# Copies of transposed keys and queries: four neighbouring words written at a time

## The chip, the cores and the metric

The program runs on one core of a Trainium2 chip. The metric is the device time of one execution in microseconds, and each kernel is given as the median of its runs. The core has a matrix engine (TensorE, PE in the profile, with its weight loads as PEld), a vector engine (VectorE, DVE), a scalar engine (ScalarE, ACT), GpSimd (POOL) and a queue engine (SyncE, SP) that issues transfers. Each engine takes its instructions in program order and waits on semaphores for the others. [...]

## The reference

```python
# B, H, S, D = 4, 8, 768, 48
mag = np.sqrt(a_re * a_re + a_im * a_im)
scale = np.minimum(mag, 0.999) / (mag + 1e-06)
a_re_n, a_im_n = (a_re * scale, a_im * scale)
for t in range(S):
    new_re = ar * S_re - ai * S_im        # ar, ai: step t of a_re_n, a_im_n
    new_im = ar * S_im + ai * S_re
    S_re, S_im = (new_re + k[t] (outer) v[t], new_im)
    y[:, :, t] = q[t] @ S_re
x = y as 3072 tokens of 384
h = x @ w_in                    # 384 x 2048
g = h * clip(h + 3, 0, 6) / 6
x = g @ w_out                   # 2048 x 384
h = x @ w_in2
g = max(h, 0) + alpha * min(h, 0)
out = g @ w_out2
```

A recurrence with complex decay per head feeds two feed-forward layers over 3072 tokens.

## The kernel before

**Work.** The 4 x 768 steps of the recurrence are handled in 12 groups of 256 tokens, each of two chunks of 128. For each group VectorE and ScalarE normalise the decay (`norm_ops`), multiply it up along time (`scan_ops`) and scale keys and queries by it, which gives the tiles `Kt` and `A`. Then `chunk_ops` does each chunk as masked attention on TensorE: transposes of keys and queries, scores `ps`, the masked product `PT`, outputs `py`, and the update `pu` of the running state `W`. The rows `xr` of a group are split into two parts (`xT`, `split_x`), and `ffn` runs the feed-forward layers: 16 steps a layer, each with matmuls into `ph` (L658), a gate on ACT and DVE (L670 to L680) that gives `gs`, and matmuls into `acc` (L695). The weights are decoded from 64-bit words once (`split_w`, `decode_f64`, mostly on DVE), stored, and fetched again for later passes (`fetch_w`).

**Order.** A list of positions (`Timeline`) sets the program order. Each group's attention steps are spread over a stretch of positions, and in between stand the steps of a feed-forward pass of earlier groups. In the first two groups there is no or little feed-forward work to stand there.

**Around the change.** A chunk's tokens lie in the tiles so that a token is t x 8 + j: 16 values of t and 8 heads give the 128 partitions, and j is the first free dimension. The helper `tr` (L563 to L568) transposes four of the eight j of one chunk with four TensorE transposes (L566) into one PSUM tile `pt` of 96 partitions x 4 x 128 words, and one ACT copy (L567) brings that to SBUF, to `KTr` or `QT`, whose 128 columns of a head are in the order of time (t outside, j inside). Each chunk has four such steps (keys half 0 and 1, queries half 0 and 1), so there are 96 copies. `pt` has one buffer (pool `ps1`, `bufs=1`), so that the next four transposes wait until the copy has read it:

```python
pt = ps1.tile([P, 4, P], F32, tag="pt", name=f"pt{n}_{g}_{half}")
...
ops += [kt0, lambda: tr(Kt, KTr, 1), lambda: tr(Qt, QT, 0), lambda: tr(Qt, QT, 1)]
```

The tag `pt` is also used for the two transposes `ptt` of `totals` (L412), for `pe` (L492) and for `gx` (L601).

Of the kernel before, what the change touches and what calls it, by code (L numbers as in the profile page):

```python
# [28 lines left out]
TB, J = 16, 8  # L29
# [190 lines left out]
def recurrence_ffn_kernel(ctx: ExitStack, tc, al, qkl, vl, w1, w2, alpha, q, k, v, a_re, a_im, out):  # L220
# [8 lines left out]
    D2 = 2 * D  # L229
# [108 lines left out]
    def grp(n):  # L338
        return divmod(n, NG)
# [213 lines left out]
    def chunk_ops(n, g, xr):  # L553
        b, cp_ = grp(n)
        c = G * cp_ + g
        Qt, Kt, V = Q_t[n], K_t[n], V_t[n]
        QT = lp.tile([D2, H, C], F32, tag="QT", name=f"QT{n}_{g}", bufs=2)
        KTr = lp.tile([D2, H, C], F32, tag="KT", name=f"KT{n}_{g}")
        KN = lp.tile([P, H, D2], F32, tag="KN", name=f"KN{n}_{g}")
        PT = [lp.tile([P, 4, C], F32, tag="PT", name=f"PT{n}_{g}_{i}", bufs=2) for i in range(2)]  # L560
        ops = []

        def tr(src, dst, half):  # L563
            pt = ps1.tile([P, 4, P], F32, tag="pt", name=f"pt{n}_{g}_{half}")
            for jj in range(4):
                nc.tensor.transpose(pt[:D2, jj], src[:, 4 * half + jj, g].rearrange("p c d -> p (c d)"), ident)  # L566
            nc.scalar.copy(  # L567
                dst.rearrange("p h (t j) -> p j (h t)", j=J)[:, 4 * half : 4 * half + 4], pt[:D2]  # L568
            )

        def natural():
            if c < NCH - 1:
                for h in range(H):
                    nc.sync.dma_start(
                        KN[:, h],
                        Kt[TB * h : TB * (h + 1), :, g].rearrange("p j c d -> p j (c d)"),
                    )

        def kt0():
            natural()  # L580
            tr(Kt, KTr, 0)

        ops += [kt0, lambda: tr(Kt, KTr, 1), lambda: tr(Qt, QT, 0), lambda: tr(Qt, QT, 1)]

        def scores(i):
            ps = ps1.tile([P, 4, C], F32, tag="ps", name=f"ps{n}_{g}_{i}")
            for hh in range(4):
                h = 4 * i + hh
                nc.tensor.matmul(ps[:, hh], lhsT=KTr[:, h], rhs=QT[:, h], start=True, stop=True)  # L589
            nc.vector.tensor_mul(PT[i], ps, mask.unsqueeze(1).broadcast_to([P, 4, C]))  # L590

        ops += [lambda: scores(0), lambda: scores(1)]

        def update():
            if c == NCH - 1:
                return
            pu = ps1.tile([P, H, D], F32, tag="ps", name=f"pu{n}_{g}")
            for h in range(H):
                nc.tensor.matmul(pu[:D2, h], lhsT=KN[:, h], rhs=V[:, g, h], start=True, stop=True)  # L599
            gx = ps1.tile([P, H], F32, tag="pt", name=f"gx{n}_{g}")  # L600
            nc.tensor.matmul(  # L601
                gx[:D2], lhsT=sel[:, g].rearrange("p c d -> p (c d)"), rhs=gam_t[n], start=True, stop=True
            )
            W = lp.tile([D2, H, D], F32, tag="W", name=f"W{n}_{g}", bufs=2)
            gb = gx[:D2].unsqueeze(2).broadcast_to([D2, H, D])
            if c == 0:
                nc.scalar.copy(W, pu[:D2])
            else:
                nc.vector.tensor_add(W, W_t[n, g], pu[:D2])
            if n < WACT:  # L610
                gs_ = lp.tile([D2, H], F32, tag="gsb", name=f"gsb{n}_{g}")
                nc.scalar.copy(gs_, gx[:D2])
                for h in range(H):
                    nc.scalar.activation(W[:, h], W[:, h], AF.Copy, scale=gs_[:, h : h + 1])
            else:
                nc.vector.tensor_mul(W, W, gb)
            W_t[(n, 1) if g == 0 else (n + 1, 0)] = W

        def outputs():
            for hp in range(H // 2):  # L620
                for par in range(2):
                    h = 2 * hp + par
                    o = py[64 * par : 64 * par + D, hp]
                    nc.tensor.matmul(o, lhsT=V[:, g, h], rhs=PT[h // 4][:, h % 4], start=True, stop=(c == 0))  # L624
                    if c > 0:
                        nc.tensor.matmul(o, lhsT=W_t[n, g][:, h], rhs=QT[:, h], start=False, stop=True)  # L626
            ys = lp.tile([P, 4, C], F32, tag="ys", name=f"ys{n}_{g}")
            nc.scalar.copy(ys, py)
            tk = slice(g * C, (g + 1) * C)
            for par in range(2):  # L630
                nc.sync.dma_start(xr[D * par : D * (par + 1), :, tk], ys[64 * par : 64 * par + D, 0:3])
            for par, e0, kk, p0, m in ((0, 0, 0, 96, 32), (0, 32, 1, 96, 16), (1, 0, 1, 112, 16), (1, 16, 2, 96, 32)):
                nc.sync.dma_start(xr[p0 : p0 + m, kk, tk], ys[64 * par + e0 : 64 * par + e0 + m, 3])

        ops += [outputs, update]
        return ops
# [212 lines left out]
```

## Time and profile before

| | before |
|---|---|
| median of 3 runs | 1198.31 us (1196.89 to 1199.21) |
| the profiled execution | 1198.93 us, of which its span 1197.2 us |
| PE busy | 1031.2 us (86%) |
| PE weight loads busy | 846.9 us (71%) |
| DVE busy | 802.1 us (67%) |
| ACT busy | 615.3 us (51%) |
| DMA, mean | 163 GB/s |

The span is the time from the first to the last instruction of the profiled execution; the time of the run has 1.7 us around it. The busy shares are means over stages that have different limits: for the first 60 us there is almost no TensorE work, later TensorE is busy nearly all the time. PE intervals are pipelined and their ends are modelled, so consecutive PE rows can overlap by some 0.2 us.

### The profile page before, as it was taken

The numbers are of one execution on the slowest core, as the hardware profiler recorded it, in microseconds if no ns is written. First come the engines' busy times: TensorE is split into PE (matmuls) and PEld (weight loads), VectorE is DVE, ScalarE is ACT, GpSimd is POOL, SyncE is SP. The second block draws the span as 40 slices with busy tenths as digits, with TensorE's granted clock in tenths as the row PEclk, the third lists the DMA queues.
The fourth block names the chain that finished last, engine by engine and source line by source line (L and its number), as shares of the span: only waits on it lengthen the run. The fifth ranks groups of instructions, "written<-read, shape, count | busy, mean of one in ns | idle before, by whom it ended". The sixth has DMA issues, their size and how long they took to land.

```text
span 1197.2 us, 15796 instructions
## 1 busy us (share of the span) xinstructions
PE 1031.2 (86%) x5914; PEld 846.9 (71%) x5914; DVE 802.1 (67%) x1537; ACT 615.3 (51%) x1003; POOL 2.0 (0%) x13
## 2 busy tenths in 40 slices
PE   0026946979998789999999999999999999999997
PEld 0015935957787787777878778778788777788786
DVE  7985973999895586948738749559579375333432
ACT  5453634667665455755356564446554346432433
POOL 0000000000000000000000000000000000000000
PEclk9999876999999899999999999999999999999999
DMA  8642472476575675445534544543454344244430
GB/s 339 253 167 61 142 303 67 134 275 194 222 247 181 213 243 178 134 128 174 171 102 153 171 120 158 193 136 116 131 188 139 130 124 138 89 163 134 133 129 30
DMA packets 70500, 194.60 MB, mean 163 GB/s; under 512 B 29456, under 2 KB 38672, under 8 KB 70416
## 3 DMA queue, kind: packets, MB, share of 16 engines
q1 hardware_dynamic: 70272, 193.50, 48.6%
q8 instruction: 49, 0.80, 0.3%
q14 instruction: 35, 0.29, 0.1%
q10 hardware_dynamic: 144, 0.01, 0.0%
HBM read 158.08 MB, written 22.81 MB: 151 GB/s over the span
## 4 chain that ended last, share of the span: by engine, by line
PE 66%; DVE 16%; ACT 12%; DMA 3%; issue 2%; SPq 0%; DVEq 0%; ACTq 0%
PE ph L658 27%; PE acc L695 24%; PE ps L589 5%; PE pt L566 4%; ACT KT L567 4%; ACT QT L567 4%; PE pu L599 3%; PE py L624 2%; DVE w L294 2%; DVE wd L76 2%; DVE wd L77 2%; PE py L626 2%; DMA w<-wsd 1%; DVE gs L680 1%; DMA A<-in_al_dram 1%
## 5 line engine op out<-in xcount | busy, mean ns | idle before, releaser
L695 PE MATMUL acc<-gs,w 128*128 128x512 f32 (+1 forms) x2016 | 453.3, 366 | 7.2 <-ACT gs L679 4.8
L695 PEld LDWEIGHTS acc<-gs,w 128*128 128x128 f32 x2016 | 335.2, 188 | 69.2 <-ACT gs L679 7.3
L658 PE MATMUL ph<-xT,w 128*128 128x256 f32 (+1 forms) x1152 | 231.2, 348 | 20.9 <-ACT xT L550 14.9
L658 PE MATMUL ph<-xs,w 128*128 128x512 f32 x864 | 224.3, 401 | 3.2 <-DVE xs L704 2.5
L658 PEld LDWEIGHTS ph<-xT,w 128*128 128x128 f32 x1152 | 185.1, 197 | 50.8 <-ACT xT L550 16.0
L658 PEld LDWEIGHTS ph<-xs,w 128*128 128x128 f32 x864 | 158.3, 188 | 40.6 <-DVE xs L704 4.0
L679 ACT CAST gs<-r 128x512 fp32r<-128x512 f32 x192 | 119.7, 624 | 119.6 <-DVE r L671 71.6
L680 DVE TENSOR_TENSOR gs<-r,gs 128x512 fp32r<-128x512 f32 x192 | 132.0, 689 | 63.5 <-ACT gs L679 63.4
L678 DVE SCALAR_TENSOR_TENSOR r<-n,nal,r 128x512 f32<-128x512 f32 x96 | 71.9, 749 | 80.9 <-ACT n L675 80.5
L670 ACT ACTIVATE r<-ph 128x512 f32<-128x512 f32 x96 | 57.3, 597 | 129.2 <-PE ph L658 128.7
L671 DVE SCALAR_TENSOR_TENSOR r<-r,ph 128x512 f32<-128x512 f32 x96 | 65.7, 684 | 83.4 <-ACT r L670 82.9
L674 ACT ACTIVATE r<-ph 128x512 f32<-128x512 f32 x96 | 57.5, 599 | 83.9 <-PE ph L658 83.1
L567 ACT COPY KT<-pt 96x512 f32<-96x512 f32 x48 | 54.8, 1143 | 47.6 <-PE pt L566 39.4
L590 DVE TENSOR_TENSOR PT<-ps,mask 128x512 f32<-128x512 f32 x48 | 33.2, 692 | 62.7 <-PE ps L589 61.0
L589 PEld LDWEIGHTS ps<-QT,KT 96*128 96x128 f32 x384 | 54.5, 214 | 21.8 <-ACT QT L567 18.5
L589 PE MATMUL ps<-QT,KT 96*128 96x128 f32 x384 | 60.5, 307 | 10.7 <-ACT QT L567 9.7
L567 ACT COPY QT<-pt 96x512 f32<-96x512 f32 x48 | 54.8, 1142 | 21.5 <-PE pt L566 21.5
L566 PE MATMUL pt<-ident,Kt 128*96 128x128 f32 x192 | 33.1, 298 | 38.0 <-DVE Kt L518 30.5
L675 ACT ACTIVATE n<-ph 128x512 f32<-128x512 f32 x96 | 57.4, 598 | 0.0
L566 PEld LDWEIGHTS pt<-ident,Kt 128*96 128x96 f32 x192 | 22.6, 136 | 48.6 <-ACT wd L73 21.2
L566 PE MATMUL pt<-ident,A 128*96 128x128 f32 x192 | 33.8, 303 | 20.9 <-ACT QT L567 10.3
L566 PEld LDWEIGHTS pt<-ident,A 128*96 128x96 f32 x192 | 20.9, 135 | 38.7 <-ACT QT L567 19.0
(107 smaller groups left out, 1054.0 us busy)
## 6 DMA issues: line engine op xcount, KB each, us to landing
w<-wsd SPq DMA_DIRECT2D x139, 768.0 KB, 4.4
raw<-in_w_dram SPq DMA_DIRECT2D x32, 768.0 KB, 5.7
wsd<-w SPq DMA_DIRECT2D x23, 768.0 KB, 4.1
A<-in_al_dram SPq DMA_DIRECT2D x12, 768.0 KB, 4.6
qk<-in_qkl_dram SPq DMA_DIRECT2D x12, 768.0 KB, 5.4
KN<-Kt SPq DMA_DIRECT2D x160, 48.0 KB, 2.3
v<-in_vl_dram SPq DMA_DIRECT2D x12, 384.0 KB, 4.4
out_dram<-o SPq DMA_DIRECT2D x18, 256.0 KB, 3.2
```

Source lines behind the costliest of these rows:

```text
L566: nc.tensor.transpose(pt[:D2, jj], src[:, 4 * half + jj, g].rearrange("p c d -> p (c d)"), ident)
L567: nc.scalar.copy(dst.rearrange("p h (t j) -> p j (h t)", j=J)[:, 4 * half : 4 * half + 4], pt[:D2])
L589: nc.tensor.matmul(ps[:, hh], lhsT=KTr[:, h], rhs=QT[:, h], start=True, stop=True)
L658: nc.tensor.matmul(ph_, lhsT=w[:, wl, kk], rhs=x[:, xl, kk], start=(kk == 0 and wl == 0 and xl == 0), stop=(kk == KT - 1 and wl == 1),)
L670: nc.scalar.activation(r, ph_, AF.Relu, bias=0.5, scale=1.0 / 6.0)
L671: nc.vector.scalar_tensor_tensor(r, r, 1.0, ph_, op0=ALU.min, op1=ALU.mult)
L674: nc.scalar.activation(r, ph_, AF.Relu)
L675: nc.scalar.activation(neg, ph_, AF.Relu, scale=-1.0)
L678: nc.vector.scalar_tensor_tensor(r[:, k], neg[:, k], nal[:, ii : ii + 1], r[:, k], op0=ALU.mult, op1=ALU.add)
L679: nc.scalar.copy(gs[:, 0], r)
L680: nc.vector.tensor_sub(gs[:, 1], r, gs[:, 0].bitcast(F32))
L695: nc.tensor.matmul(acc, lhsT=w[:, wl, e * P : (e + 1) * P], rhs=gs[:, gl], start=(i == 0 and wl == 0 and gl == 0), stop=(i == NF - 1 and g ...
```

## The change

The ACT copy of `tr` reads and writes the same words as before and puts each to the same place. Only the order in which it walks them differs. Before, the outer loop is j (four) and the inner loop the 128 columns of one transpose: it reads PSUM in four runs of 128 neighbouring words, and each word is written 8 words (32 bytes) behind the one before. After, the outer loop is the 128 columns and the inner loop the four j: it writes runs of four neighbouring words (16 bytes), with 32 bytes from one run to the next, and reads each word of a run 128 words (512 bytes) behind the one before, in PSUM.

```diff
             nc.scalar.copy(
-                dst.rearrange("p h (t j) -> p j (h t)", j=J)[:, 4 * half : 4 * half + 4], pt[:D2]
+                dst.rearrange("p h (t j) -> p (h t) j", j=J)[:, :, 4 * half : 4 * half + 4],
+                pt[:D2].rearrange("p j x -> p x j"),
             )
```

The number of instructions and their order are as before on every engine; on ACT only the shape of the 96 copies is another (96x128x4 for 96x4x128). Lines behind L567 have a number that is higher by one.

## Rows read from the trace of the kernel before

**Rows 1.** The page's head and its part 1, busy time by engine.

```profile
span 1197.2 us, 15796 instructions
PE 1031.2 (86%) x5914; PEld 846.9 (71%) x5914; DVE 802.1 (67%) x1537; ACT 615.3 (51%) x1003; POOL 2.0 (0%) x13
```

**Rows 2.** Stretches: length, busy us (instructions) by engine, PE clock, DMA share, GB/s.

```profile
60.00:240.00 180.00, 119.55 (x849) 108.67 (x850) 131.15 (x251) 89.23 (x153) 0.00 (x0) 0.86 0.44 146
240.00:480.00 240.00, 213.38 (x1458) 181.74 (x1457) 191.61 (x372) 141.44 (x240) 0.00 (x0) 0.99 0.65 218
480.00:1080.00 600.00, 586.27 (x3133) 467.56 (x3132) 389.23 (x748) 312.52 (x499) 0.00 (x0) 1.00 0.45 143
```

**Rows 3.** Shares of the chain that ended last, by line, from the page.

```profile
PE ph L658 27%; PE acc L695 24%; PE ps L589 5%; PE pt L566 4%; ACT KT L567 4%; ACT QT L567 4%; PE pu L599 3%; PE py L624 2%; DVE w L294 2%; DVE wd L76 2%; DVE wd L77 2%; PE py L626 2%; DMA w<-wsd 1%; DVE gs L680 1%; DMA A<-in_al_dram 1%
```

**Rows 4.** Groups of ACT by shape: count, busy us, mean ns, idle before, releaser.

```profile
L567 ACT COPY KT<-pt 96x512 f32<-96x512 f32 x48 | 54.8, 1143 | 47.6 <-PE pt L566 39.4 <-PE ps L589 8.0
L567 ACT COPY QT<-pt 96x512 f32<-96x512 f32 x48 | 54.8, 1142 | 21.5 <-PE pt L566 21.5
L73 ACT ACTIVATE wd<-raw 128x768 f32<-128x768 f32 x32 | 29.1, 911 | 19.3 <-DVE w L294 16.8 <-DMA raw<-in_w_dram 2.4
...
L628 ACT COPY ys<-py 128x512 f32<-128x512 f32 x24 | 14.1, 587 | 33.7 <-PE py L626 26.0 <-PE py L624 5.6 <-DMA w<-wsd 1.8
...
L528 ACT ACTIVATE Ts<-Ts 128x768 f32<-128x768 f32 x12 | 10.1, 845 | 0.1
```

**Rows 5.** Line L567, 60 to 240 us: durations, and who waited (us, times).

```profile
L567 ACT COPY KT<-pt x8: 1069/1092/1100, 79.3 to 187.8; 96x512 f32<-96x512 f32 x8
...
  PE pt L566: 13.3, 11
...
  PE ps L589: 4.6, 4
```

**Rows 6.** The same line, 240 to 480 us: who waited.

```profile
  PE pt L566: 5.8, 15
...
  PE ps L589: 2.0, 5
```

**Rows 7.** The same line, 480 to 1080 us: durations, and who waited.

```profile
L567 ACT COPY KT<-pt x28: 1132/1155/1247, 508.4 to 1034.0; 96x512 f32<-96x512 f32 x28
...
  PE pt L566: 7.7, 23
  PE ps L589: 3.0, 8
...
  PE ptt L412: 1.1, 3
```

**Rows 8.** Timeline of PE around one copy: start, length, what, idle before, releaser.

```profile
622.79 1.18 PE L695 MATMUL acc<-gs,w 128*128 128x512 f32 x4
624.28 0.64 PE L566 MATMUL pt<-ident,A 128*96 128x128 f32 x4 [0.31 <-ACT KT L567]
```

**Rows 9.** Timeline of ACT at the same place.

```profile
623.07 1.16 ACT L567 COPY KT<-pt 96x512 f32<-96x512 f32 x1 [0.77 <-PE pt L566]
```

**Rows 10.** The chain in order of time, a stretch with no wait: start, length, what.

```profile
640.15 2.10 PE acc L695 x9
```

**Rows 11.** Timeline of PE in the first group's attention.

```profile
82.78 1.09 PE L566 MATMUL pt<-ident,A 128*96 128x128 f32 x4 [1.19 <-ACT KT L567]
```

**Rows 12.** Waits of PE, 130 to 200 us: in total, times, longest.

```profile
PE pt L566 <- DVE Kt L518: 9.7, 1, 9.7
```

**Rows 13.** A stretch of the weight decoding, columns as in the second group.

```profile
240.00:300.00 60.00, 50.62 (x285) 38.82 (x284) 56.78 (x83) 42.24 (x70) 0.00 (x0) 1.00 0.69 234
```

**Rows 14.** Waits of PE for the copies, 240 to 300 us: in total, times, longest.

```profile
PE pt L566 <- ACT QT L567: 0.7, 2, 0.3
PE pt L566 <- ACT KT L567: 0.3, 1, 0.3
```

## The prediction

> **What bounds the kernel now.** I read the busy times first: PE is busy 86% of the span, more than any other engine [rows 1]. Then the stretches, because that share is a mean over stages. From 480 to 1080 us PE is busy 586.27 of 600 us at a granted clock of 1.00: TensorE sets the pace, and what it loses there, 13.7 us in all, lengthens the program. From 60 to 240 us it is busy only 119.55 of 180 us, and between 240 and 480 us 213.38 of 240 us, so other things hold it up there [rows 2]. The chain that ended last says where the copies stand: keys and queries take 4% of the span each, some 96 us, although the 96 copies last only 109.6 us altogether (54.8 and 54.8) [rows 3, 4]. So nearly every copy is on the path.
>
> Next, the groups by shape. A copy takes 1143 ns for 512 words of 96 partitions; the copy of `py` at L628, which also moves 512 words a partition from PSUM to SBUF but reads and writes them side by side, takes 587 ns [rows 4]. The 556 ns between them are 1.09 ns for each word that is written 32 bytes behind the last one. That is what the change goes for.
>
> Last, who waits for the copies. PE idles for them 13.3 + 4.6 = 17.9 us in 15 waits from 60 to 240 us [rows 5], 5.8 + 2.0 = 7.8 us in 20 waits from 240 to 480 us [rows 6], and 7.7 + 3.0 + 1.1 = 11.8 us in 34 waits from 480 to 1080 us [rows 7]: there it is most of the 13.7 us that PE loses.
>
> **What one wait is worth.** At 622.79 four matmuls of the feed-forward start, and the transposes behind them start at 624.28 [rows 8]. Without a wait nine such matmuls take 2.10 us, 0.233 each [rows 10], so the transposes could start at 622.79 + 4 x 0.233 = 623.72: 0.56 us are lost, though the row says 0.31 idle, since the modelled end of a matmul lies behind the time at which the next could start. The copy runs from 623.07 to 624.23 [rows 9]. A copy shorter by up to 0.56 us thus gives all of it back to this wait. In the first groups the wait is longer, 1.19 us, because nothing stands between two sets of transposes [rows 11]: there any shortening counts in full.
>
> **The cost of a copy after.** No row shows an engine that reads PSUM in steps, so I bound it from both sides.
> - Write side: with four words side by side, at best nothing is left of the 556 ns; at worst each of the 128 jumps still pays 1.09 ns, 0.14 us.
> - Read side, below: nothing, 0.587 us for the copy, the duration of L628. A price below that has no reason: it moves as many words a partition.
> - Read side, above: each word read 512 bytes behind the last pays what a word written in steps pays now, 1.09 ns: 0.587 + 0.556 = 1.14 us, as before. It could be more; that is the slower rival below.
> - Nearest row of a read in steps on ACT: the activation at L73 takes every second word of `raw`, 911 ns for 768 words, against 845 ns for the one at L528, which reads them side by side [rows 4]. That is 66 ns, 0.086 ns a word, 0.045 us for 512.
>
> I take that row, since it is the same engine and the same side of the instruction, though it reads SBUF and in steps of 8 bytes: 0.587 + 0.045 = 0.63 us. A copy gets shorter by 1.155 - 0.63 = 0.52 us in the late stretch, by about 0.51 from 240 to 480, and by 1.08 - 0.63 = 0.45 in the early one, where those of keys take 1.07 to 1.10 us [rows 5, 7].
>
> For the write side the rows above show only the price of single words at 32 bytes. [...]
>
> [...] The read now is in four runs of 128 neighbouring words, and no row shows one in steps. [...]
>
> **The sum.**
> - 480 to 1080 us: 34 waits x 0.52 = 17.7 us. At least the idle time shown, 11.8.
> - 240 to 480 us: VectorE is busy 56.78 of the 60 us up to 300 us, among other things with decoding weights [rows 13], so I count nothing for the three waits of that stretch, 0.7 + 0.3 us [rows 14]; the other 17 give 17 x 0.51 = 8.7 us. At least their idle time, 7.8 - 1.0 = 6.8.
> - 60 to 240 us: 15 waits x 0.45 = 6.8 us. Between the first two groups TensorE waits 9.7 us for `Kt` from VectorE [rows 12]. VectorE takes its work in order and itself waits for scores in the first group's attention, so it should get ahead by the same time and hand most of it on; if it does not, half is lost, 3.4.
> - After 1080 us no copy is left (the last of keys starts at 1034.0 [rows 7]). No other instruction changes. ACT is freed of some 50 us, for which nothing is added, as its 51% does not bound.
>
> Together 33.2 us. The profiled execution took 1198.93 us (span 1197.2 and 1.7 around it): 1165.7, and as that execution lies 0.6 above the median of the runs, I say **1165 us** (2.8% less). Its own range is 1155 to 1177: the low end if waits that show only on the weight loads give something too and the first groups' attention speeds up further, the high end if only the idle times count (11.8 + 6.8 + 3.4 = 22.0 us), about the same as where the jumps of the write keep their 0.14 us.
>
> **The rivals.**
> 1. *The read eats half.* The copy ends midway between the bounds, at 0.87 us, 0.28 shorter late and 0.21 early: 34 x 0.28 + 17 x 0.27 + 15 x 0.21 = 17 us, **1181 us**. For it: the step is 64 times that of L73, and no two words are neighbours. Against: PSUM is read here by one engine at a time, and nothing in the trace shows what would hold it up. [...]
> 2. *One penalty for another.* A word read in steps costs as much as one written in steps, 1.09 ns. The copy stays at 1.14 us, and the time at **1198 us**. For it: the write shows that ACT can lose more than a word's time per step, and why should a read be better. [...]
> 3. *Slower.* The read pays more than the write does now; the point from which this decides is 1.09 ns a word. At twice that the copy takes 0.587 + 1.11 = 1.70 us, 0.56 more. The 66 waits counted above grow by that, 37 us, and of the 27 copies that PE does not wait for today perhaps half their surplus shows, 27 x 0.28 = 8: **1243 us**. For it: the step keeps to four places 512 bytes apart in the same 2 KB of PSUM, so that each read goes elsewhere. Against: it needs a step twice as dear as the dearest that the trace has.
> 4. *The copies shrink, but another wait takes their place early*: only the late stretch gives, 17.7 us, **1181 us**. For it: VectorE is nearly full from 240 to 300 us [rows 13]. Against: all copies of the first groups lie on the chain.
>
> **How the numbers follow.** Forecast 0.48, rival 1 0.15, rival 2 0.14, rival 3 0.15, rival 4 0.08. The likeliest case alone gives 1155 to 1177. The range takes in rivals 1, 2 and 4, to hold 8 in 10: 1153 to 1204. A measurement of this kernel tells about 0.2%, 2.4 us, from no change, that is 0.04 us a copy. Of rival 2 I put 0.08 within that, 0.02 faster, 0.04 slower. Faster: 0.48 + 0.15 + 0.08 + 0.02 = 0.73, which I lower to 0.70, since rival 1 reaches down to nothing; same 0.09; slower 0.21.
>
> **What would show it.** The mean of the two L567 groups is the first thing to look at: near 0.63 us the forecast, 0.87 rival 1, 1.14 rival 2, over 1.2 rival 3. Then the idle time of PE before L566, L589 and L412 for copies: it should fall from 11.8 us to under 2 us in the late stretch, and by 0.45 us a wait in the first groups. If the copies are short and the time between the start of the first `Kt` transposes and the second group's does not shrink by some 3 us, rival 4 is right there. The prediction is wrong, above all, if a PSUM read in steps of 512 bytes is dear, which nothing in this trace can exclude.

## The result, and the profile after

The changed kernel takes **1158.68 us** (median of 6 runs, 1157.46 to 1159.72) against 1198.53 us of the kernel before (median of 6 runs): a ratio of 0.9668, with a 95% interval of 0.9656 to 0.9681. That is 39.9 us less, where 33 were forecast, and inside the forecast's own range of 1155 to 1177.

The page's head and its busy times, which answer to [rows 1]:

```profile
span 1155.8 us, 15796 instructions
PE 1017.3 (88%) x5914; PEld 846.7 (73%) x5914; DVE 799.6 (69%) x1537; ACT 567.4 (49%) x1003; POOL 2.0 (0%) x13
```

The span is 41.4 us shorter and ACT has 47.9 us less to do; the number of instructions is the same on every engine. The groups of ACT by shape answer to [rows 4]:

```profile
L567 ACT COPY QT<-pt 96x512 f32<-96x512 f32 x48 | 28.1, 586 | 20.5 <-PE pt L566 20.4
L567 ACT COPY KT<-pt 96x512 f32<-96x512 f32 x48 | 28.0, 583 | 46.0 <-PE pt L566 38.3 <-PE ps L590 7.7
L629 ACT COPY ys<-py 128x512 f32<-128x512 f32 x24 | 14.1, 586 | 34.1 <-PE py L627 28.2 <-PE py L625 5.9
```

The copies took 1143 and 1142 ns before; now, at 586 and 583 ns, they last as long as the copy of `py`, which reads and writes everything side by side (586 ns). Nothing is left of the 556 ns that the write cost, and the read, in which the words of a run of four lie 512 bytes apart, adds nothing that can be seen beside those 586 ns.

Who waits for line L567 now, from 60 to 240 us (answers to [rows 5]), from 240 to 480 us ([rows 6]) and from 480 to 1080 us ([rows 7]), in us and times:

```profile
  PE pt L566: 8.9, 10
...
  PE ps L590: 2.7, 4
...
  PEld pt L566: 2.3, 12
  PEld ps L590: 1.1, 5
...
  PEld pt L566: 4.8, 23
  PEld ps L590: 2.0, 8
  PEld ptt L412: 0.7, 3
```

In the first stretch PE still idles 11.6 us for the copies, 6.3 less than the 17.9 before; the place of [rows 11] now shows 0.67 us of idle time for 1.19:

```profile
81.88 1.09 PE L566 MATMUL pt<-ident,A 128*96 128x128 f32 x4 [0.67 <-ACT KT L567]
```

In the two later ones there is no row of PE at all: only weight loads still start a little late, while the matmul before them is running. The timeline of PE around one set of transposes shows what has become of the place in [rows 8]:

```profile
596.86 1.18 PE L696 MATMUL acc<-gs,w 128*128 128x512 f32 x4
597.88 0.60 PE L566 MATMUL pt<-ident,A 128*96 128x128 f32 x4
```

The transposes start 1.02 us after the four matmuls, where it was 1.49 us. The copy in between, in the timeline of ACT, ends at 597.73:

```profile
597.14 0.59 ACT L567 COPY KT<-pt 96x512 f32<-96x512 f32 x1 [0.77 <-PE pt L566]
```

The stretches (length, busy us and instructions of PE, PEld, DVE, ACT and POOL, clock, DMA share, GB/s), beside [rows 2]:

```profile
60.00:240.00 180.00, 123.34 (x897) 112.40 (x898) 139.86 (x264) 86.05 (x160) 0.00 (x0) 0.85 0.48 162
240.00:480.00 240.00, 223.90 (x1492) 191.59 (x1492) 201.52 (x389) 140.41 (x258) 0.00 (x0) 0.99 0.64 216
480.00:1080.00 600.00, 599.68 (x3228) 487.22 (x3228) 381.77 (x737) 280.32 (x493) 0.00 (x0) 1.00 0.45 148
```

From 480 to 1080 us PE is now busy 599.68 of 600 us, and does 3228 matmuls in them instead of 3133. The granted clock is the same as before in each stretch within 0.01. The chain's shares by line, beside [rows 3], say it from the other side: no copy is left among the lines listed.

```profile
PE ph L659 30%; PE acc L696 29%; PE ps L590 4%; PE pt L566 4%; PE py L625 2%; PE pu L600 2%; DVE w L294 2%; DVE wd L76 2%; PE py L627 2%; DVE wd L77 1%; DMA w<-wsd 1%; DVE gs L681 1%; DVE wd L74 1%; DMA raw<-in_w_dram 1%; DVE r L672 1%
```

Where along the way the time is gained shows at fixed places of the program: the transposes `ptt` of the third group's scan and of the sixth's, first of the kernel before, then of the changed one (line, count, ns least/median/most, first to last start).

```profile
L412 PE MATMUL ptt<-ident,tot x2: 417/446/474, 196.4 to 196.7; 128*128 128x128 f32 x2
...
L412 PE MATMUL ptt<-ident,tot x2: 272/272/273, 470.9 to 471.0; 128*128 128x128 f32 x2
```

```profile
L412 PE MATMUL ptt<-ident,tot x2: 421/448/474, 187.8 to 188.1; 128*128 128x128 f32 x2
...
L412 PE MATMUL ptt<-ident,tot x2: 270/271/272, 450.9 to 451.0; 128*128 128x128 f32 x2
```

The lead is 8.6 us after the first two groups, 20.0 us at the sixth group, and 41.4 at the end (of these two executions; between the medians it is 39.9).

### The profile page after: what moved, and what is told of

The parts are those of the page before. It is cut to its first block, busy times and chain, and to the rows that moved or that the text cites. A ratio compares the mean times of both kernels' runs of the same rounds, so it can differ in the third digit from the quotient of the medians.

```text
span 1155.8 us, 15796 instructions
## 1 busy us (share of the span) xinstructions
PE 1017.3 (88%) x5914; PEld 846.7 (73%) x5914; DVE 799.6 (69%) x1537; ACT 567.4 (49%) x1003; POOL 2.0 (0%) x13
## 4 chain that ended last, share of the span: by engine, by line
PE 75%; DVE 16%; ACT 3%; DMA 3%; issue 2%; SPq 1%; DVEq 0%; ACTq 0%
PE ph L659 30%; PE acc L696 29%; PE ps L590 4%; PE pt L566 4%; PE py L625 2%; PE pu L600 2%; DVE w L294 2%; DVE wd L76 2%; PE py L627 2%; DVE wd L77 1%; DMA w<-wsd 1%; DVE gs L681 1%; DVE wd L74 1%; DMA raw<-in_w_dram 1%; DVE r L672 1%
## 5 line engine op out<-in xcount | busy, mean ns | idle before, releaser
L567 ACT COPY KT<-pt 96x512 f32<-96x512 f32 x48 | 28.0, 583 | 46.0 <-PE pt L566 38.3
L396 DVE TENSOR_TENSOR m<-A 128x384 f32<-128x384 f32 x84 | 46.8, 557 | 1.9
L508 DVE TENSOR_TENSOR Ts<-A,EL 128x1536 f32<-128x1536 f32 x24 | 42.1, 1754 | 0.7 <-ACT EL L495 0.7
L625 PE MATMUL py<-PT,v 128*48 128x128 f32 x384 | 42.0, 300 | 0.2 <-DVE PT L591 0.2
```

## The experiments

**Theory and rivals.** Theory 1: the gain is the time for which the next transposes wait for the one PSUM tile that the copy is reading. The rival: ACT had less to do, so that its gates and other copies came earlier. A second question is what a walk costs, by its jumps, by whether neighbours follow one another, or by which words fall into the same 16 bytes. Each kernel is compared with runs of the kernel before that were taken beside it; their median was 1198.72 us beside e1 to e4, 1198.32 beside e5 to e8 and 1197.12 beside e9 to e11.

**e1_refill: give ACT the work back.**

```diff
                 pt[:D2].rearrange("p j x -> p x j"),
             )
+            pad = lp.tile([D2, 100, 4], F32, tag="pad", name=f"pad{n}_{g}_{half}")
+            nc.scalar.copy(pad, dst.rearrange("p h (t j) -> p (h t) j", j=J)[:, :100, 4 * half : 4 * half + 4])
```

> The changed kernel, and behind each of the 96 copies ACT does a second copy of 400 words (of what was just written, into a tile that nothing reads), about 0.5 us, so that ACT is about as busy as before the change while the PSUM tile is released as early as after it. Theory 1, the gain is the shorter time for which the next transposes wait for the PSUM tile: the time stays near that of the changed kernel, 1158 to 1168 us. Rival, the gain is ACT's freed time (48 us of ACT work less, so that gates and other copies on ACT run earlier): most of it is lost again, 1185 to 1200 us.

Measured: 1149.01 us (1145.77 to 1153.13), ratio 0.957 (0.9549 to 0.9592). With 96 more copies it is not slower than the changed kernel but 10 us faster, which neither theory allows. ACT is busy 609.4 us in it, against 615.3 before the change and 567.4 after, and its groups are as meant:

```profile
L567 ACT COPY QT<-pt 96x512 f32<-96x512 f32 x48 | 28.1, 585 | 7.3 <-PE pt L566 7.3
L567 ACT COPY KT<-pt 96x512 f32<-96x512 f32 x48 | 28.0, 583 | 39.1 <-PE pt L566 33.0 <-PE ps L592 6.1
L572 ACT COPY pad<-QT 96x400 f32<-96x400 f32 x48 | 25.3, 527 | 0.8
L572 ACT COPY pad<-KT 96x400 f32<-96x400 f32 x48 | 25.2, 526 | 1.1
```

But its matmuls were faster. In the chain in order of time of the changed kernel nine matmuls of the feed-forward take 2.10 us, and in this kernel 2.04:

```profile
1060.52 2.10 PE ph L659 x9
1062.62 2.10 PE acc L696 x9
```

```profile
1060.54 2.04 PE acc L698 x9
1062.58 2.04 PE ph L661 x9
```

Two things differed besides the copies: a tile of 1600 bytes moves the tiles behind it in SBUF, and a few matmuls stand in another order. So the run said nothing until it had a control.

**e5_shift: the control, the place alone.** The tile is set aside, and no copy uses it; the order of all other instructions is that of the changed kernel.

```diff
+            if (n, g, half) == (0, 0, 0) and src is Kt:
+                pad = lp.tile([D2, 400], F32, tag="pad", name="pad")
+                nc.gpsimd.memset(pad[:, 0:1], 0.0)
```

> The control for the kernel with the second copies: the changed kernel with the same 1600 bytes a partition set aside in SBUF, without the copies (one word of it is set once by GpSimd); all other instructions stand as in the changed kernel, and the tiles xT, xs, gs, r, ys, W and A lie 1600 bytes higher. In the kernel with the second copies nine feed-forward matmuls took 2.04 us in the late stretch, 2.10 in all others. Theory P, that is the place of the moved operands: 2.04 us here too, and 2880 matmuls of 512 columns at 6.6 ns less give about 19 us, 1140 us; the second copies then cost about 9 us, and ACT's time is a small part of the gain. Rival, it came with the order or the copies: 2.10 us and 1157 to 1160 us.

Measured: 1148.51 us (1147.36 to 1149.68), ratio 0.9585 (0.9565 to 0.9605). The chain again has nine matmuls in 2.04 us:

```profile
1061.32 2.04 PE ph L662 x9
1063.36 2.04 PE acc L699 x9
```

So it was the place, though it is worth 10 us and not the 19 expected. Against this control the 96 second copies of e1, 50.5 us of ACT's time, cost 0.5 us, less than the runs scatter (1145.77 to 1153.13 in e1). The two differ besides in the order of a few matmuls, whose share was not measured by itself. The rival, by which e1 should have taken 1185 us or more, is refuted: ACT's time was not what the kernel lacked.

**e6_shift_old_walk and e7_shift64.** The same tile in the kernel before, and 64 bytes instead of 1600 in the changed kernel.

> The kernel before with the same 1600 bytes set aside. Theory P: the place works without the new walk, about 19 us off, 1178 to 1182 us, and the new walk is worth about the same 40 us at either place. Rival: no change, 1196 to 1200 us.

> The changed kernel with 64 bytes set aside instead of 1600. If any move of the tiles serves, nine matmuls take 2.04 us and the time is about 1140 us; if it hangs on where exactly the operands lie, 2.10 us and 1157 to 1160 us, or slower.

Measured: 1186.84 us (1184.77 to 1188.34), ratio 0.9906 (0.9885 to 0.9927), and 1147.71 us (1145.30 to 1150.94), ratio 0.9584 (0.9559 to 0.961). The place gives 11.5 us with the old walk and 10.2 to 11.0 with the new one, and 64 bytes do as well as 1600. The two shifts differ by 1536 bytes, three times 512, so they place a tile alike with respect to any power of two up to 512 bytes: the runs do not tell whether any move would serve. At the moved place the new walk is worth 1186.84 - 1148.51 = 38.3 us, near the 39.9 at the old place, so the two add up, and the gain of the change is its own.

**e2_late: the new walk in groups 5 to 11 alone.**

```diff
+            if n >= 5:
                 (new walk)
+            else:
                 (old walk)
```

> The new walk only in groups 5 to 11, whose attention runs beside the long feed-forward passes; groups 0 to 4 keep the old walk. Theory 1, each shortened wait is worth its 0.56 us wherever it stands, and the trace of the changed kernel puts 21 us of its 40 into this part: 1177 us. By the terms of the prediction, 34 waits at 0.52 us, 17.7 us: 1181 us. Rival, the late gain is only work that has been moved ahead by the early groups' gain: less than 10 us, above 1188 us.

Measured: 1176.51 us (1174.47 to 1178.64), ratio 0.981 (0.9787 to 0.9832). The late groups' copies give 22.2 us, and by difference the first five groups' 17.7. The late part stands on its own and is no echo of the early one. The early groups alone were not run, so their part is what is left of the whole.

**e4_two_tiles_old_walk: the old copies, but two PSUM tiles in turn.**

```diff
-            pt = ps1.tile([P, 4, P], F32, tag="pt", ...)
+            pt = ps1.tile([P, 4, P], F32, tag=("pt", "ps")[half], ...)
```

> The old walk, with copies of 1.15 us, but the second half of each transposed tile goes to another PSUM tile (that of the scores), so that four transposes need not wait for the copy just ahead of them. Theory 1, what the old copies cost was the wait for the one PSUM tile: much of the gain comes without any change of the copy, 1170 to 1188 us; not all, because scores and transposes now share a tile and the copies still follow one another on ACT. Rival, what counts is how long ACT works: no gain, 1195 to 1200 us. Some instructions beside the transposes change places in the order as well.

Measured: 1176.55 us (1173.37 to 1178.43), ratio 0.9814 (0.9796 to 0.9833). With copies that are no faster (they take 1161 and 1167 ns), more than half of the gain is there. That is theory 1 from the other side, with the reservation that some other instructions changed places too. What is left of PE's waits for them from 480 to 1080 us:

```profile
PE ps L589 <- ACT QT L567: 4.0, 11, 0.8
PE ptt L412 <- ACT KT L567: 1.5, 3, 0.5
```

The transposes of keys and queries are no longer held up there; the totals `ptt`, which use the tile `pt` too, and the scores, which need the last copy itself, still are.

**e3_pairs and e9_skip: what the write pays for.** e3 writes two neighbouring words at a time, e9 two words of the same 16 bytes that are 8 bytes apart.

```diff
-                dst.rearrange("p h (t j) -> p (h t) j", j=J)[:, :, 4 * half : 4 * half + 4],
-                pt[:D2].rearrange("p j x -> p x j"),
+                dst.rearrange("p h (t j2 i) -> p j2 (h t) i", j2=J // 2, i=2)[:, 2 * half : 2 * half + 2],   # e3
+                pt[:D2].rearrange("p (j2 i) x -> p j2 x i", i=2),                                            # e3
+                dst.rearrange("p h (t j i) -> p i (h t) j", j=J // 2, i=2)[:, :, :, 2 * half : 2 * half + 2], # e9
+                pt[:D2].rearrange("p (j i) x -> p i x j", i=2),                                              # e9
```

> All copies walk so that two neighbouring words are written at a time (8 bytes, the next pair 32 bytes on) and two words 512 bytes apart are read. Theory A, a write that has a neighbour in its run costs nothing extra, whatever the length of the run: copies of 0.59 us and 1158 to 1160 us. Theory B, every jump of the write costs the 1.09 ns that single words paid: 256 jumps of 512 words give 0.59 + 0.28 = 0.87 us and about 1178 us. Theory C, a run must fill 16 bytes to be free: the copy is at 1.0 us or more, above 1185 us.

> The walk writes two words that lie in the same 16 bytes but are not neighbours (8 bytes apart), and then goes on 32 bytes; pairs of neighbours at the same distance took 0.66 us a copy and 1163.7 us. Theory L, it counts that two words fall into the same 16 bytes: about 0.66 us a copy and 1162 to 1166 us. Theory N, it counts that the next word is the neighbour: about 1.1 us a copy and 1190 to 1200 us.

Measured: e3 1163.67 us (1163.37 to 1165.25), ratio 0.9701 (0.9685 to 0.9717); e9 1162.04 us (1158.20 to 1163.20), ratio 0.9699 (0.9679 to 0.9719). The copies of e3, then of e9:

```profile
L567 ACT COPY QT<-pt 96x512 f32<-96x512 f32 x48 | 32.0, 666 | 20.7 <-PE pt L566 20.7
L567 ACT COPY KT<-pt 96x512 f32<-96x512 f32 x48 | 31.8, 663 | 46.2 <-PE pt L566 38.5 <-PE ps L590 7.7
```

```profile
L567 ACT COPY QT<-pt 96x512 f32<-96x512 f32 x48 | 32.0, 666 | 20.7 <-PE pt L566 20.7
L567 ACT COPY KT<-pt 96x512 f32<-96x512 f32 x48 | 31.6, 658 | 46.4 <-PE pt L566 38.6 <-PE ps L590 7.7
```

For e3 none of the three theories held exactly: two words at a time leave 0.08 us of the 0.56, not nothing and not half. e9 agrees with theory L and refutes theory N: the two words need not be neighbours if they fall into the same 16 bytes (658 and 666 ns a copy, where pairs of neighbours take 663 and 666). Whether the 16 bytes count, or only that the hop between the two is 8 bytes and not 32, no run separates; nor does one tell the price of a jump in the write from that of a shorter inner loop of the walk. With steps of 32 bytes, as here, a write that goes on to other 16 bytes after each word pays 1.09 ns a word, after two words 0.08 us / 256 = 0.3 ns a jump, after four nothing.

**e8, e10 and e11: a version that beats both.** e8 is the new walk with two tiles in turn (the edit of e4); e11 adds the 64 bytes of e7; e10 has the 64 bytes and takes the second tile in groups 0 to 4 only:

```diff
-            pt = ps1.tile([P, 4, P], F32, tag="pt", ...)
+            pt = ps1.tile([P, 4, P], F32, tag="ps" if half and n < 5 else "pt", ...)
```

> The new walk, and every second set of transposes goes to the PSUM tile of the scores. Theory 1: what is left of PE's waits for the copies, 11.6 us of idle time in the first two groups and nothing later, can be shortened: up to 8 us, 1151 to 1158 us. Rival: the tile shared with the scores makes waits of its own, as in the kernel with the old walk, 1159 to 1166 us.

> New walk, 64 bytes set aside, and in groups 0 to 4 every second set of transposes in the tile of the scores (in the kernel that did so in all groups the lead over the changed kernel was 10 us at the fifth group's attention and fell to 6 by the end). If the three add up: 1158.7 - 11 - 10 = 1138 us, at least below 1144; if the tile's gain is absorbed by the decoding of weights, 1147 us.

> The same with the second tile in all groups: 1158.7 - 11 - 6 = 1142 us if they add up, and slower than with it in the early groups only.

Measured: e8 1152.59 us (1150.65 to 1153.78), ratio 0.9619 (0.9598 to 0.9641); e10 **1138.93 us** (1137.23 to 1141.24), ratio 0.9512 (0.9496 to 0.9528); e11 1141.71 us (1140.31 to 1143.12), ratio 0.9538 (0.9522 to 0.9554). e8 lies in the range of theory 1. The three measures add up: e10 and e11 were expected at 1138 and 1142 us. In e10 the transposes of queries no longer wait for copies from 60 to 240 us, where they did for 7.6 us in all in the changed kernel (groups of PE, e10 and then the changed kernel, whose waits of this kind all lie in that stretch):

```profile
L569 PE MATMUL pt<-ident,A 128*96 128x128 f32 x40 | 8.6, 364 | 3.7 <-ACT gsb L616 3.5 <-issue 0.2
```

```profile
L566 PE MATMUL pt<-ident,A 128*96 128x128 f32 x192 | 31.5, 290 | 7.6 <-ACT QT L567 4.6 <-ACT KT L567 3.0
```

What they wait for now is the copy `gsb` from the same tile, 3.5 us.

## Why the prediction was right, point by point

- **What bounds.** Right. From 480 to 1080 us PE now has next to nothing to wait for (busy 599.68 of 600 us). That nearly every copy was on the path went too far: the prediction's own count has 69 waits of PE for 96 copies. That the wait for the tile and not ACT's time was the cost is shown by e1 against e5 on one side and by e4 on the other, each within the reservation stated there.
- **The cost of a copy.** Forecast 0.63 us, measured 0.583 to 0.586. The term that was mis-sized is the price of the read, taken as 0.045 us from an SBUF read in steps of 8 bytes; it is nothing that shows. The write lost its whole price of 556 ns at four words, as in the better of the two bounds. No two consecutive words of the read are neighbours, and the copy takes what L629 takes, 586 ns. No row of the kernel before shows that the write would keep none of its 556 ns (by the rows up to 0.14 us could stay), and the forecast counts on it; the runs show nothing left at four words (583 and 586 ns a copy) and 0.08 us at two (e3).
- **One wait is worth the copy's shortening.** Right in mechanism: at the place of [rows 8] 1.49 us became 1.02, against 0.93 with no wait at all, so 0.47 us of the copy's 0.57 came back there. In the first group, at the place of [rows 11], 1.19 us of idle time became 0.67: the whole 0.5 us by which the copy is shorter there.
- **480 to 1080 us.** Forecast 17.7 us, e2 gives 22.2 (20.1 to 25.5 by its interval). With the copy as measured, 34 waits x 0.568 us make 19.3; with the 0.47 us seen at the one place above, 16.0. The rest, 3 to 6 us, may be waits that the count left out: 47 weight loads waited for copies in that stretch before (33 + 11 + 3), PE's matmuls only 34 times. That part is reckoned, not shown by a run.
- **60 to 480 us.** Forecast 8.7 + 6.8 = 15.5 us, by difference of e2 17.7, in the two traces 20.0 up to 470 us. With 0.50 us in place of 0.45 a wait, and 0.56 in place of 0.51, the forecast's own counts make 7.5 + 9.5 = 17.0. VectorE handed the first group's time on: PE waits the same 9.7 us for `Kt` as before [rows 12], and that wait ends 5.6 us sooner after the first `Kt` transposes than it did (85.23 us for 90.83). First the kernel before, then the changed one:

```profile
78.25 1.06 PE L566 MATMUL pt<-ident,Kt 128*96 128x128 f32 x4 [20.84 <-DVE Kt L518]
...
169.08 1.06 PE L566 MATMUL pt<-ident,Kt 128*96 128x128 f32 x4 [9.66 <-DVE Kt L518]
```

```profile
78.39 1.06 PE L566 MATMUL pt<-ident,Kt 128*96 128x128 f32 x4 [20.85 <-DVE Kt L518]
...
163.62 1.06 PE L566 MATMUL pt<-ident,Kt 128*96 128x128 f32 x4 [9.69 <-DVE Kt L518]
```

- **The rivals.** Half eaten, one penalty for another, and slower all hung on the read, and fall with it. The fourth, an early gain taken by VectorE, falls by the sign that the prediction gave for it: the time between the two groups' `Kt` transposes shrinks by 5.6 us, not by less than some 3. What was said against the first, that PSUM is read by one engine at a time, is not so: in the kernel before, ACT copies `pt` while DVE reads `ph`, both in PSUM, and the copy takes 1.16 us, where the median of the `QT` copies from 480 to 1080 us is 1.154:

```profile
608.37 1.16 ACT L567 COPY QT<-pt 96x512 f32<-96x512 f32 x1
608.51 0.69 DVE L671 SCALAR_TENSOR_TENSOR r<-r,ph 128x512 f32<-128x512 f32 x1 [4.28 <-ACT r L670]
```

- **How much was luck.** The mechanism is the one forecast. The total came out 6.7 us low (33.2 for 39.9): the read was priced too high, and, as far as is known, the late waits were counted too few. The 0.52 us taken for a late wait, where 0.47 was seen at the one place worked out, errs the other way, so a part of the nearness may be luck. That the read costs next to nothing was a choice between bounds that no row could decide, as the prediction says itself.

## What to carry to other kernels

In this kernel a copy by ACT that reorders 4-byte words cost by its side in SBUF: 1143 ns with each word written 32 bytes behind the last, 0.66 us with two words of the same 16 bytes written in turn, and 583 to 586 ns with four, though the four were read 512 bytes apart in PSUM. So for such a copy try the order of loops in which the words that fall into the same 16 bytes are written one after the other and the PSUM side does the jumping; here that took 0.56 us off each of 96 copies. Then ask what waits for the copy: a PSUM tile with one buffer can make the copy's length a wait of TensorE, as it was here at 69 of 96 copies, although ACT was busy only 51% of the time. And a control with the same memory layout belongs to every experiment that adds a tile, since the layout alone moved this kernel by 10 to 11.5 us, 1%.

## What the runs showed that was not expected

Where the tiles behind `PT` lie in SBUF mattered here. With them 64 or 1600 bytes higher, and the instructions otherwise in the same order, nine matmuls of 512 columns take 2.04 us instead of 2.10 at about the same granted clock (means of 0.971 to 0.973, against 0.972 to 0.975 without the move), and the program 10 to 11.5 us less, with either walk. Expected were 2880 x 6.6 ns = 19 us. Matmuls of 256 columns gained nothing: those into `acc` have a mean of 281 ns in the changed kernel and 285 in e5, those into `ph` 297 and 302, which would take some 5 us back; the means rest on modelled ends. The gain comes late: at the sixth group's `ptt` the kernel of e5 stands at 453.6 us, 2.6 behind the changed kernel's 450.9, and at the end it is 10.1 ahead. Which tile it is (`xT`, `xs` and `gs` are read, others move with them) and what about its address counts was not tried, nor a shift that is not 64 bytes more than a multiple of 512.

Reading PSUM 512 bytes further from word to word of a run of four cost ACT nothing that shows (583 and 586 ns for 512 words, where the copy of `py`, side by side, takes 586).
